# Slabs of four (entry, head) pairs interleaved by partition, with wq in the same ring of buffers

## The chip, the core and the metric

The kernel runs on one core of a Trainium2 chip. TensorE (PE) multiplies matrices, VectorE (DVE) and ScalarE (ACT) work element by element, GpSimd (POOL) only fills constants here, and SyncE (SP) issues the transfers from the chip's memory. A transfer is cut into packets, which 16 DMA engines carry. The core's SBUF has 128 partitions; matrix products land in PSUM. The metric is the device time of one execution in microseconds (us), lower is better.

## The reference

Two independent problems, A and B, have the same shapes, and their results stand side by side. Each is one decode step of attention over the last 4,096 positions of a cache, with 2 batch entries, 32 query heads and 16 key/value heads of 128 elements:

```python
W = min(4096, max(256, Sk // 4))                      # Sk = 16384
q = (x @ wq).reshape(B, Sq, Hq, Dh).transpose(0, 2, 1, 3)   # x: 2 x 1 x 576
k = jnp.repeat(k_cache[:, :, Sk - W:, :], rep, axis=1)      # rep = 2
v = jnp.repeat(v_cache[:, :, Sk - W:, :], rep, axis=1)
p = softmax(einsum("bhqd,bhkd->bhqk", q, k) * Dh ** -0.5)
o = einsum("bhqk,bhkd->bhqd", p, v)
return o.transpose(0, 2, 1, 3).reshape(B, Sq, Hq * Dh) @ wo   # wo: 4096 x 576
```

All arrays are bf16. K and V of the window are 134 MB of the 153.1 MB that the profile counts as read.

## The kernel before

Each (entry, head) pair needs 1 MB of K and 1 MB of V. A slab of 2 MB holds one key/value head for both entries: row `r` of 64 rows of 16 KB and entry `b` stand in partition `2r + b` (line 255). There are 32 slabs of K and 32 of V. They pass through a ring of 5 buffers (`NR`, line 77) in the order K0, K1, ..., K5, V0, K6, V1, ..., so that V runs `LS` = 5 slabs behind K (lines 227 to 231). Slab `s` takes buffer `s % 5` and waits for the last reader of slab `s - 5` (lines 258 to 260).

All loads but x stand in SP's queue in one fixed order, which `ensure_stream_until` (line 300) writes out. wq has buffers of its own, four loads of 1 MB in rows of 8 KB (line 282) and one of 0.5 MB (line 283). wo comes in 8 parts of 1,152 KB, one for each group of 8 pairs; a part fills `wob` with 128 rows of 9,216 bytes (lines 296 and 297), or for the last group with pieces of 1,152 bytes. The last V slab is cut into four pieces (`PIECES`, line 98).

For a K slab DVE transposes 32x32 blocks of 4-byte words, 512 words per partition at a time (line 844), and PE multiplies the result with `zq`, in which the queries stand so that each product adds into the right rows of a score bank (`fS`, line 867; its moving operand takes every fourth 2-byte element). After 8 units, that is 4 slabs, a group is complete: its maximum, exponent and sum pass through DVE, PE and ACT (`c_max` to `c_gather`, lines 373 to 493). V is multiplied four matmuls side by side, 16 columns of `pC` each (line 786); ACT or DVE copies the bank out (lines 802 and 804), PE adds its parts (line 758), DVE normalizes (line 561), and `redist`, `rev` and `gproj` (lines 630 to 665) apply wo. Every engine runs its instructions in the order in which the lists `S.add` were filled, and waits on semaphores for the others.

The new file is a rewrite of this plan with its own line numbers; these are given with the diff.

Of the kernel before, what the change touches and what calls it, by code (L numbers as in the profile page):

```python
# [59 lines left out]
def build_kernel(nc, probs, out, cfg=None):  # L60
    cfg = dict(cfg or {})
    NR = cfg.get("NR", 5)
    NKT = cfg.get("NKT", 3)
    NTB = cfg.get("NTB", 2)
    NZQ = 2
    ZW = 144
    LAG = cfg.get("LAG", 11)
    NPT = 3
    NS = cfg.get("NS", 56)
    LS = cfg.get("LS", 5)  # L70
    WQ_AT = cfg.get("WQ_AT", 7)
    QP_AT = cfg.get("QP_AT", 24)
    WO_LEAD = cfg.get("WO_LEAD", 5)
# [9 lines left out]
    NJ = W // 128  # L83
    assert NJ == 32
    NQ = 4
    NJ2 = 2 * NJ
    NRW = 64
    SLABW = NJ2 * 128
    UW = NJ * 128
    PP = Bb * Hkv  # L90
    NP = PP * NPROB
    ND = NP // 2
    NG = NP // 8
    GPP = PP // 8
    KP = PP // 2
    NK = NP // 2
    NFC = D // 128
    DREM = D - 128 * NFC
    assert DREM * 2 == 128
    HH = HD // 2  # L100
    NCH = NFC + 1
    NXC = NFC + 2
    NOUT = wo0.shape[1]
    NH = (NOUT + 1) // 2
    ACC0 = 128
    assert NOUT % 2 == 0 and ACC0 + NH <= 512 and NS <= 64 and NS % 2 == 0
    SCALE = float(Dh) ** -0.5
    PW = 512
    PIECES = [(0, 32), (32, 48), (48, 56), (56, 64)]

    def slab_info(D_):
        return D_ // Hkv, D_ % Hkv
# [5 lines left out]
    with es:  # L118
# [3 lines left out]
        xt = sb("xt", [128, NKT, UW], BF16)  # L122
        wqb = sb("wqb", [128, NFC, HD], BF16)
        wqr = sb("wqr", [128, HH], BF16)
        wob = sb("wob", [128, 2, 8, NOUT], BF16)
        xT = sb("xT", [128, NPROB, NXC, 64], BF16)
        x_dup = sb("x_dup", [Bb, NPROB, 2, DREM, 2], BF16)
        x_sb = sb("x_sb", [Bb, NPROB, D], BF16)
        ident_b = sb("ident_b", [128, 192], BF16)
        zq = sb("zq", [128, 4, NZQ, 8, ZW], BF16)  # L130
        pR = sb("pR", [128, 2, PW], BF16)
        pT = sb("pT", [128, 2, 2 * PW], BF16)
# [3 lines left out]
        sel = sb("sel", [128, 4, 128], BF16)  # L136
        qT_sb = sb("qT_sb", [128, NG, 64], BF16)
# [8 lines left out]
        oTn = sb("oTn", [128, 2, 2, Bb], BF16)  # L146
# [3 lines left out]
        maskS = sb("maskS", [128, 8], BF16)  # L150
        selL = sb("selL", [128, 240], BF16)
        acc_sb = sb("acc_sb", [128, 2, 512], BF16)
        ident_r = sb("ident_r", [128, 72], BF16)
        pC = sb("pC", [128, NPT, 4, 2, NJ, 4], BF16)
        mask_bh = sb("mask_bh", [128, Bb, 2], BF16)
        out_sb = sb("out_sb", [Bb, NPROB, NOUT], BF16)
        ps = lambda name, shape: es.enter_context(nc.psum_tensor(name, shape, FP32))
        TB = [ps("tb%d" % i, [128, 512]) for i in range(NTB)]
        assert NTB == 2
# [9 lines left out]
        x_sems = [sem("xload%d" % P) for P in range(NPROB)]  # L169
        out_sem = sem("outdone")  # L170
        lastq_sem = [sem("lastq%d" % q_) for q_ in range(4)]
# [10 lines left out]
        p_ones_b = S.add("pool", lambda e: e.memset(ones_b[:], 1.0), [], "ones_b")  # L182
        def f_identb(e):
            e.affine_select(ident_b[:, 0:128], ones_b[:], [[-1, 128]], ALU.is_equal, 0.0, base=0, channel_multiplier=1)
            return e.memset(ident_b[:, 128:192], 0.0)
        p_ident_b = S.add("pool", f_identb, [p_ones_b], "ident_b")
        p_zqT = S.add("pool", lambda e: e.memset(qT_sb[:].rearrange("d g w -> d (g w)"), 0.0), [], "zero_qT")
        p_zxT = S.add("pool", lambda e: e.memset(xT[:].rearrange("c p h w -> c (p h w)"), 0.0), [], "zero_xT")

        def zq_zero(eng, zr_, p4s, tag):  # L190
            ops_ = []
            for p4 in p4s:
                ops_.append(S.add(eng, lambda e, p4=p4: e.memset(zq[:, p4, zr_, :, :].rearrange("d l w -> d (l w)").bitcast(FP32), 0.0),
                                  [], "%s_%d" % (tag, p4)))
            return ops_
        p_zq = {0: zq_zero("pool", 0, (2, 3), "zero_zq0p")}

        def f_sel(e):
            last = None
            for p4 in range(4):  # L200
                b32, par = p4 // 2, p4 % 2
                last = e.affine_select(sel[:, p4, :].rearrange("d (a p) -> d a p", a=4), ones_b[:, :].rearrange("d (a p) -> d a p", a=4),
                                       [[0, 4], [-2, 32]], ALU.is_equal, 0.0, base=-(64 * b32 + par), channel_multiplier=1)
            return last
        p_sel = S.add("pool", f_sel, [p_ones_b], "sel")
        p_ones_f = S.add("pool", lambda e: e.memset(ones_f[:], 1.0), [], "ones_f")
        p_ident_f = S.add("pool", lambda e: e.affine_select(ident_f[:], ones_f[:], [[-1, 128]], ALU.is_equal, 0.0,
                                                           base=0, channel_multiplier=1), [p_ones_f], "ident_f")
        for zr_ in range(1, NZQ):
            p_zq[zr_] = zq_zero("pool", zr_, (0, 1, 2, 3), "zero_zq%d" % zr_)  # L210

        p_zq[0] = p_zq[0] + zq_zero("dve", 0, (0, 1), "zero_zq0d")
        init_zero = {}
        init_zero["ST0"] = S.add("dve", lambda e: e.memset(ST[0][:], 0.0), [], "zero_ST0")
        late_zero = [("ST1", ST[1]), ("OT0", OT[0]), ("OT1", OT[1]), ("ACC0", ACC[0]), ("ACC1", ACC[1])]

        x_sem = x_sems[0]

# [7 lines left out]
        stream = []  # L226
        for s_ in range(ND + LS):
            if s_ < ND:
                stream.append(("K", s_))
            if s_ >= LS:  # L230
                stream.append(("V", s_ - LS))
        slab_idx = {key: n for n, key in enumerate(stream)}
        w_at = {}
        for P in range(NPROB):
            t0 = 0 if P == 0 else WQ_AT + 4 * GPP * (P - 1)
            for ch in range(NCH):
                w_at.setdefault(t0 + (0 if P == 0 else ch), []).append(("wq", P, ch))
        for G in range(NG):
            w_at.setdefault(4 * G + LS + (2 if by_group(G) else -1), []).append(("wo", G, 0))

        slab_dma = {}
        slab_quarters = {}
        slab_last_reader = {}
        wq_dma = {}
        wo_dma = {}
        qproj = {}
        qproj_ev = {}
        proj = {}
        next_stream = [0]

        def issue_slab(s):
            kind, D_ = stream[s]
            P, g = slab_info(D_)
            src_t = probs[P][1] if kind == "K" else probs[P][2]
            src = src_t[:, g, Sk - W:Sk, :].rearrange("b (r j) d -> r b (j d)", r=NRW)
            r = s % NR
            deps = []
            if s >= NR:
                assert slab_last_reader.get(s - NR) is not None, ("ring too small / order", s)
                deps = [slab_last_reader[s - NR]]  # L260

            if s == len(stream) - 1:
                qops = []
                for n_, (ja, jb) in enumerate(PIECES):
                    def fq(e, r=r, src=src, n_=n_, ja=ja, jb=jb):
                        return e.dma_start(ring[:, r, ja * 128:jb * 128], src[:, :, ja * 128:jb * 128]).then_inc(lastq_sem[n_], 16)
                    qops.append(dma_op("sp", lastq_sem[n_], 1, fq, deps, "%s%d_q%d" % (kind, D_, n_)))
                slab_dma[s] = qops[-1]
                slab_quarters[s] = qops
                return  # L270

            def f(e, r=r, src=src):
                return e.dma_start(ring[:, r, :], src).then_inc(ring_sem[r], 16)
            slab_dma[s] = dma_op("sp", ring_sem[r], 1, f, deps, "%s%d" % (kind, D_))

        def issue_wq(P, ch):
            wqP = probs[P][3]
            deps = [qproj[P * GPP - 1]] if P >= 1 else []

            def f(e):  # L280
                if ch < NFC:
                    return e.dma_start(wqb[:, ch, :], wqP[ch * 128:(ch + 1) * 128, :]).then_inc(wq_sem[P], 16)
                return e.dma_start(wqr[:, :], wqP[NFC * 128:D, :].rearrange("r (h n) -> r h n", h=2)).then_inc(wq_sem[P], 16)
            wq_dma[(P, ch)] = dma_op("sp", wq_sem[P], 1, f, deps, "wq%d_%d" % (P, ch))

        def issue_wo(G):
            P = G // GPP
            Gl = G % GPP
            woP = probs[P][4]
            h0 = Gl * 8  # L290
            pc = G % 2
            deps = [proj[4 * (G - 2) + 3]] if G >= 2 else []

            def f(e):
                rows = woP[h0 * 128:(h0 + 8) * 128, :]
                src = rows.rearrange("(p s) n -> p s n", s=8) if by_group(G) else rows.rearrange("(h d) n -> d h n", d=128)
                return e.dma_start(wob[:, pc, :, :], src).then_inc(wo_sem[pc], 16)
# [42 lines left out]
        def group_of(i):  # L340
            return i // 8
# [652 lines left out]
```

## Time and profile before

| what | us |
|---|---|
| median of 3 runs | 372.18 (372.13 to 372.52) |
| the profiled execution, its own time | 373.62 |
| its span on the core | 371.8 |
| PE busy in the span | 313.2 |
| DVE busy in the span | 213.4 |
| ACT busy in the span | 30.4 |

The profile is of one execution. Its page cuts the span into 40 slices of 9.3 us and gives for each the share of time that engines were busy and the GB/s that the DMA engines moved. A group line gives the program line, the engine, the operation, the tiles and shapes, a count, the busy time, the mean of one in ns, and the idle time ahead with what ended it. "SPq" is SP's queue of transfers. The packet records of the trace hold start, duration and size of each packet; a semaphore's records hold when each part of a transfer reported that it had landed.

### The profile page before, as it was taken

The numbers are of one execution on the slowest core, as the hardware profiler recorded it, in microseconds if no ns is written. First come the engines' busy times: TensorE is split into PE (matmuls) and PEld (weight loads), VectorE is DVE, ScalarE is ACT, GpSimd is POOL, SyncE is SP. The second block draws the span as 40 slices with busy tenths as digits, with TensorE's granted clock in tenths as the row PEclk, the third lists the DMA queues.
The fourth block names the chain that finished last, engine by engine and source line by source line (L and its number), as shares of the span: only waits on it lengthen the run. The fifth ranks groups of instructions, "written<-read, shape, count | busy, mean of one in ns | idle before, by whom it ended". The sixth has DMA issues, their size and how long they took to land.

```text
span 371.8 us, 4249 instructions
## 1 busy us (share of the span) xinstructions
PE 313.2 (84%) x1764; PEld 97.3 (26%) x1764; DVE 213.4 (57%) x433; ACT 30.4 (8%) x99; POOL 6.5 (2%) x21
## 2 busy tenths in 40 slices
PE   0249997999899498999899878999699878998576
PEld 0214422222232134332223212322223222232132
DVE  3089638837853557545875557645775557726412
ACT  1100101010101001010101001010101001000111
POOL 7000000000000000000000000000000000000000
PEclk9998998999899699999989996999889996898769
DMA  7999999999999999999999999999999999999993
GB/s 310 435 430 428 427 420 361 391 386 434 420 435 428 427 425 427 420 429 428 430 429 421 428 434 425 422 432 427 425 427 430 425 427 427 425 429 413 434 414 120
DMA packets 13172, 153.39 MB, mean 413 GB/s; under 512 B 1368, under 2 KB 2400, under 8 KB 3040
## 3 DMA queue, kind: packets, MB, share of 16 engines
q1 hardware_dynamic: 13144, 153.10, 97.9%
q8 instruction: 14, 0.23, 0.3%
q14 instruction: 6, 0.05, 0.0%
q10 hardware_dynamic: 8, 0.00, 0.0%
HBM read 153.10 MB, written 0.00 MB: 412 GB/s over the span
## 4 chain that ended last, share of the span: by engine, by line
PE 46%; DMA 37%; DVE 13%; ACT 1%; issue 1%; SPq 1%
PE st L867 34%; DMA ring<-in_B_k_cache_dram 22%; DMA ring<-in_A_k_cache_dram 10%; DVE xt L844 8%; DMA ring<-in_B_v_cache_dram 5%; PE acc L786 4%; PE ot L658 3%; DVE pT L476 2%; PE tb L513 2%; DVE m L378 1%; DVE pC L491 1%; ACT pR L428 1%; PE tb L407 1%; PE tb L452 1%; PE tb L382 1%
## 5 line engine op out<-in xcount | busy, mean ns | idle before, releaser
L867 PE MATMUL st<-xt,zq 128*128 128x512 bf16 x512 | 236.0, 606 | 27.1 <-DVE xt L844 27.1
L844 DVE STREAM_TRANSPOSE xt<-ring 128x512 f32<-128x512 f32 x256 | 158.8, 675 | 53.5 <-DMA ring<-in_B_k_cache_dram 24.5
L867 PEld LDWEIGHTS st<-xt,zq 128*128 128x128 bf16 x512 | 48.9, 109 | 152.4 <-issue 108.2
L786 PE MATMUL acc<-ring,pC 128*16 128x512 bf16 x508 | 43.0, 412 | 3.5 <-DMA ring<-in_B_v_cache_dram 3.3
L561 DVE TENSOR_TENSOR oTg<-ot,rsb 128x4 bf16<-128x4 f32 x28 | 4.3, 152 | 38.0 <-PE ot L758 38.0
L802 ACT ACTIVATE acc_sb<-acc 128x512 bf16<-128x512 f32 x16 | 9.6, 597 | 143.0 <-PE acc L786 143.0
L804 DVE CAST acc_sb<-acc 128x512 bf16<-128x512 f32 x16 | 10.9, 678 | 15.1 <-PE acc L786 15.1
L476 DVE STREAM_TRANSPOSE pT<-pR 128x1024 bf16<-128x1024 bf16 x8 | 10.0, 1246 | 12.4 <-ACT pR L428 12.4
L513 PE MATMUL tb<-xT,wqb 128*128 128x56 bf16 x256 | 11.1, 198 | 6.5 <-DMA wqr<-in_A_wq_dram 6.5
L658 PE MATMUL ot<-wob,Rsb 128*2 128x288 bf16 x112 | 16.2, 302 | 0.3 <-ACT Rsb L646 0.3
L786 PEld LDWEIGHTS acc<-ring,pC 128*16 128x16 bf16 x508 | 7.9, 86 | 30.9 <-issue 23.8
L758 PEld LDWEIGHTS ot<-ident_r,acc_sb 128*128 128x128 bf16 x132 | 8.7, 106 | 20.8 <-issue 11.3
L513 PEld LDWEIGHTS tb<-xT,wqb 128*128 128x128 bf16 x256 | 10.8, 103 | 10.4 <-DMA wqr<-in_A_wq_dram 6.6
L658 PEld LDWEIGHTS ot<-wob,Rsb 128*2 128x2 bf16 x112 | 9.3, 88 | 10.1 <-issue 5.1
L378 DVE TENSOR_REDUCE m<-st 128x1 f32<-128x512 f32 x8 | 5.3, 667 | 9.7 <-PE st L867 9.7
L758 PE MATMUL ot<-ident_r,acc_sb 128*128 128x56 bf16 x132 | 9.7, 197 | 1.1 <-ACT out_sb L676 0.5
L513 PE MATMUL tb<-xT,wqr 128*128 128x56 bf16 x64 | 10.2, 197 | 0.0
L382 PE MATMUL tb<-ident_f,m 128*1 128x128 f32 x8 | 2.3, 283 | 8.6 <-DVE m L378 8.6
L545 ACT ACTIVATE zq<-tb 32x64 bf16<-32x64 f32 x32 | 7.1, 220 | 11.7 <-PE tb L527 11.5
L362 PE MATMUL tb<-ident_b,x_sb 2*128 2x2 bf16 x8 | 0.4, 161 | 7.5 <-DVE x_dup L348 7.5
L513 PEld LDWEIGHTS tb<-xT,wqr 128*128 128x128 bf16 x64 | 6.6, 103 | 0.0
L517 ACT ACTIVATE qT_sb<-tb 128x16 bf16<-128x16 f32 x8 | 1.5, 183 | 60.4 <-PE tb L513 60.4
(63 smaller groups left out, 84.6 us busy)
## 6 DMA issues: line engine op xcount, KB each, us to landing
ring<-in_A_k_cache_dram SPq DMA_DIRECT2D x16, 2048.0 KB, 18.0
ring<-in_A_v_cache_dram SPq DMA_DIRECT2D x16, 2048.0 KB, 16.7
ring<-in_B_k_cache_dram SPq DMA_DIRECT2D x16, 2048.0 KB, 17.6
ring<-in_B_v_cache_dram SPq DMA_DIRECT2D x15, 2048.0 KB, 19.0
wob<-in_A_wo_dram SPq DMA_DIRECT2D x4, 1152.0 KB, 17.1
wob<-in_B_wo_dram SPq DMA_DIRECT2D x4, 1152.0 KB, 16.9
wqb<-in_A_wq_dram SPq DMA_DIRECT2D x4, 1024.0 KB, 7.9
wqb<-in_B_wq_dram SPq DMA_DIRECT2D x4, 1024.0 KB, 15.7
```

The lines of the kernel that those rows point to most:

```text
L378: chain[(G, "max")] = S.add("dve", lambda e: e.tensor_reduce(m1[:], ST[x][:, :], AX.X, ALU.max), deps, "cmax_%d" % G)
L382: n, bank, op = tb_job(lambda e, bank: e.transpose(bank[0:1, 0:128], m1[:, 0:1], ident_f[:]), "cTm_%d" % G, [chain[(G, "max")], p_ident_f])
L476: return e.transpose(pT[:, G % 2, :], src)
L513: last = e.matmul(bank[:, hl * 64:hl * 64 + NS], w_, x_, start=(ch == 0), stop=(ch == NCH - 1))
L545: last = e.activation(dst, src, ACTF.Copy)
L658: last = e.matmul(OT[half][0:Bb, ACC0:ACC0 + NH], Rsb[:, G % 2, s_, :], wob[:, G % 2, s_, half * NH:(half + 1) * NH], start=False, stop=Tr ...
L758: last = e.matmul(OT[x][:, 0:NS], acc_sb[:, x, 128 * jl4:128 * jl4 + 128], ident_r[:, 4 * jl4:4 * jl4 + NS], start=False, stop=True, skip_ ...
L786: last = e.matmul(ACC[x][32 * cb:32 * cb + 16, 0:512], pC[:, pr, gl, jh, jl:jl + 4, :].rearrange("k j c -> k (j c)"), ring[:, r, j0_ * 128 ...
L802: acc_ev[D_] = S.add("act", lambda e: e.activation(acc_sb[:, x, :], ACC[x][:, :], ACTF.Copy), d, "accev_%d" % D_)
L804: acc_ev[D_] = S.add("dve", lambda e: e.tensor_copy(acc_sb[:, x, :], ACC[x][:, :]), d, "accev_%d" % D_)
L844: xop = S.add("dve", lambda e, r=r, c=c, q=q, o=o: e.transpose(xt[:, c, q * 1024:(q + 1) * 1024].bitcast(FP32), ring[:, r, o:o + 1024].bit ...
L867: last = e.matmul(ST[x][:, 0:512], zq[:, p4, zr, 2 * gl + b, 16 - 16 * jh:144 - 16 * jh], mv, start=False, stop=True, skip_group_check=True)
```

## The change

Slabs are now 4 MB and hold four pairs: heads `g` and `g + 8` of both entries. Row `r` of 32 rows of 32 KB and pair `c` stand in partition `4r + c`. There are 16 slabs of K and 16 of V, V two slabs behind K, in a ring of 3 buffers. The first 512 rows of wq also come through this ring, as one load of 4 MB, ahead of K0 for A and ahead of K3 for B; the buffers `wqb` are gone.

The transposition takes 1,024 words per instruction and writes each pair to a place of its own, so consecutive words that it writes lie 2,048 bytes apart (`[128, 2, 2, 4, 64, 8]`, the fourth index is the pair). The matmul for the scores then reads every second 2-byte element of one pair. q is projected with x as the stationary operand and 512 columns of wq moving, and is brought into place by a DVE transposition and copies. A group is two slabs; because the groups now hold heads from the two halves of the 32 query heads, a part of wo is two runs of 512 rows, half of wo apart. As built, the source of this load is 2 by 64 rows of 4,608 elements, its destination 128 partitions; before, both sides were 128 by 4,608. The last part of wo is two loads. PV uses 32 columns of `pC`; only ACT copies its bank out. The last V slab is cut into five pieces. The output leaves in four transfers.

```diff
-    NR = cfg.get("NR", 5)
-    LS = cfg.get("LS", 5)
+    NR = cfg.get("NR", 3)
+    LS = 2
+    WQ_AT = cfg.get("WQ_AT", 3)
...
-    PIECES = [(0, 32), (32, 48), (48, 56), (56, 64)]
+    PIECES = [(0, 64), (64, 96), (96, 112), (112, 120), (120, 128)]
...
-        xt = sb("xt", [128, NKT, UW], BF16)
-        wqb = sb("wqb", [128, NFC, HD], BF16)
+        xt = sb("xt", [128, 2, 2, 4, 64, 8], FP32)
...
+        for s_ in range(ND + LS):
+            if s_ == 0 or s_ == WQ_AT:
+                stream.append(("Q", 0 if s_ == 0 else 1))
+            if s_ < ND:
+                stream.append(("K", s_))
+            if s_ >= LS:
+                stream.append(("V", s_ - LS))
+        for G in range(NG):
+            s_ = 2 * G + LS if by_group(G) else 2 * G + 1
+            w_at.setdefault(("K", s_) if s_ < ND else ("V", s_ - LS), []).append(G)
...
-            src = src_t[:, g, Sk - W:Sk, :].rearrange("b (r j) d -> r b (j d)", r=NRW)
-            r = s % NR
+            src = src_t.rearrange("b h s d -> (b h) s d")[g::SPP, Sk - W:Sk, :].rearrange("c (r j) d -> r c (j d)", r=32)
+            r = n % NR
+            deps = [reader[n - NR]] if n >= NR else []
...
+        def issue_wq(n, P):
+            deps = [reader[n - NR]] if n >= NR else []
+            slab_dma[n] = dma_op("sp", ring_sem[r], 1, lambda e: e.dma_start(
+                ring[:, r, :], wqP[0:NFC * 128, :].rearrange("(p s) n -> p (s n)", s=NFC)).then_inc(ring_sem[r], 16), deps, "wq%d" % P)
...
         def issue_wo(G):
-            deps = [proj[4 * (G - 2) + 3]] if G >= 2 else []
-                rows = woP[h0 * 128:(h0 + 8) * 128, :]
-                src = rows.rearrange("(p s) n -> p s n", s=8) if by_group(G) else rows.rearrange("(h d) n -> d h n", d=128)
-                return e.dma_start(wob[:, pc, :, :], src).then_inc(wo_sem[pc], 16)
+            deps = [proj[2 * (G - 2) + 1]] if G >= 2 else []
+                if by_group(G):
+                    src = woP.rearrange("(t r) n -> t r n", t=2)[:, r0:r0 + 512, :].rearrange("t (p s) n -> t p (s n)", s=8)
+                    return e.dma_start(wob[:, pc, :, :].rearrange("p s n -> p (s n)"), src).then_inc(wo_sem[pc], 16)
+                for t in range(2):
+                    src = woP[t * HH + r0:t * HH + r0 + 512, :].rearrange("(h d) n -> d h n", d=128)
+                    last = e.dma_start(wob[:, pc, 4 * t:4 * t + 4, :], src).then_inc(wo_sem[pc], 16)
...
+        def do_X(s, u):
+                    src = ring[:, n % NR, o:o + 4096].bitcast(FP32).rearrange("k (j f w) -> k f j w", f=2, w=32)[:, hf]
+                    dst = xt[:, bf, hf, :, 32 * q:32 * q + 32, :].rearrange("k c j r -> k j r c")
+                    return e.transpose(dst, src)
+        def do_S(s, u):
+                        mv = xt[:, bf, hf, c, :, :].rearrange("k j r -> k (j r)").bitcast(BF16).rearrange(
+                            "k (n t) -> k n t", t=2)[:, :, par]
...
+        for s in range(ND + 1):
+            D2 = s - 3
...
+                for c in range(NU):
+                    do_X(s, c)
+                    if c >= 1:
+                        do_S(s, c - 1)
...
+                    if D2 >= 0:
+                        if c == 0:
+                            do_comb(D2)
+                        elif c == 1:
+                            do_norm(D2)
+                        elif c == 2 and D2 % 2 == 1:
+                            do_redist(D2 // 2)
+                        elif c == 3 and D2 % 2 == 1:
+                            do_proj(D2)
...
+                    if s == WQ_AT:
+                        do_qproj(GPP + c)
+                do_S(s, NU - 1)
+                if s % 2 == 1:
+                    do_max(s // 2)
+                    do_exp(s // 2)
+                if s >= LS:
+                    do_PV(s - LS, range(NRD), None)
+                if s % 2 == 1:
+                    do_sum(s // 2)
```

In the new file the slab load is line 231, that of wq line 238, the parts of wo lines 253 and 257, the pieces line 228, the transposition line 410 and the score matmul line 433.

## The prediction

> **What bounds the kernel now.** I read the slices first, then the transfer queues, the transfers one kind at a time, the waits of SP's queue, and the groups of instructions.
>
> ```profile
> DMA  7999999999999999999999999999999999999993
> DMA packets 13172, 153.39 MB, mean 413 GB/s; under 512 B 1368, under 2 KB 2400, under 8 KB 3040
> q1 hardware_dynamic: 13144, 153.10, 97.9%
> ...
> L867 PE MATMUL st<-xt,zq 128*128 128x512 bf16 x512 | 236.0, 606 | 27.1 <-DVE xt L844 27.1
> L844 DVE STREAM_TRANSPOSE xt<-ring 128x512 f32<-128x512 f32 x256 | 158.8, 675 | 53.5 <-DMA ring<-in_B_k_cache_dram 24.5
> ...
> L658 PE MATMUL ot<-wob,Rsb 128*2 128x288 bf16 x112 | 16.2, 302 | 0.3 <-ACT Rsb L646 0.3
> ```
>
> The 16 DMA engines are full in every slice but the first and the last: packets take 97.9% of 371.8 us, 364.0 us on each engine, and 7.8 us are left for the head and the tail. The chain of waits gives PE 46%, but PE and DVE wait for slabs (24.5 us of DVE's idle time ahead of L844 is K of B), not the slabs for them. So what counts is the work of the fullest DMA engine, plus the time in which it has nothing issued.
>
> ```profile
> wob<-in_A_wo_dram SPq DMA_DIRECT2D x4, 1152.0 KB, 17.1
> wob<-in_B_wo_dram SPq DMA_DIRECT2D x4, 1152.0 KB, 16.9
> ...
> out_dram<-out_sb SPq DMA_DIRECT2D x2, 2.2 KB
> x_sb<-in_A_x_dram ACTq DMA_DIRECT2D x1, 2.2 KB
> ```
>
> The second line of the first fence counts 1,368 packets under 512 B. They are the reports of landing. There are 85 transfers with 128 rows (63 slabs, 4 pieces, 10 parts of wq, 8 of wo) and 4 with two rows (x and the output): 85 x 16 + 4 x 2 = 1,368. So a transfer does not always use 16 engines: these four used two each, and the landing records of their semaphores say the same. The packet records give the prices: 620 ns on average for 16,384 B (median 613), 319 for 8,192, 351 for 9,216, 161 for 4,096, 85 for 2,048, 51 for 1,152.
>
> **The change, on the transfers.** Slabs: 31 whole ones, each 8 packets of 32 KB per engine. No row has such a packet. As two of 16 KB it costs 1,240 ns; growing as the medians do from 309 to 613 it costs 613 + 2 x 304 = 1,221. I take 1,240, since hardware may cut it in two: 31 x 8 x 1.240 = 307.5 us (302.8 by the other). The five pieces: 8 x (0.620 + 0.319 + 0.161 + 2 x 0.085) = 10.2. wq: 2 x 8 x 1.240 = 19.8, its rest 2 x 8 x 0.161 = 2.6. The last part of wo: 64 x 0.051 = 3.3. Reports: about 0.5. That is 343.9 us per engine, without the seven other parts of wo.
>
> Those seven are what I expect to decide. Before, a part was 128 rows on 16 engines: 8 x 0.351 = 2.8 us each. Now its source is 2 by 64 rows, while the destination still counts 128 partitions. Every other large load keeps 32 or 128 in front, and 64 in front (the old slabs) used 16 engines. The lower bound is that 128 partitions decide, 2.8 us; the upper one is that the 2 in front decides, as in x and the output, the only rows with a 2 in front: 64 rows on each of two engines, 64 x 0.351 = 22.5 us. I take the upper one, the row it is nearest to in what differs. Then two engines carry 7 x 22.5 = 157.2 us of wo instead of 19.7, and in all 343.9 + 157.2 = 501.1 us. Every slab needs all 16 engines, so these two set the pace.
>
> [...]
>
> Two engines now write into all 128 partitions, where the other 14 land their slabs. In the trace each engine always delivers about 26 GB/s (16,384 B in 620 ns) to its own 8 of the 128 rows, so it does not say whether the engine or the partitions limit this. Bounds for a wo packet beside moving slabs: 351 ns, or 702 if two writers share one writer's rate. The slots say how long the others move during a part: after it starts on the slow engines they get V (K's slot free after X) and then K (V's slot free after PV), 2 x 9.9 = 19.8 us. Shared fully a part takes about 9 us more, not shared 0. I take 550 ns in those stretches, nearer to 702 because no row shows more than that rate into a partition group: in 19.8 us then go packets worth 19.8 x 351 / 550 = 12.6 us, so a part takes 7.2 us more, 50 us in all.
>
> [...]
>
> **Waits on the transfer queue.** Nothing waits while the two slow engines have work queued. Between two parts they carry four slabs, 4 x 9.9 = 39.7 us, and a part: a period of 62 us or more, eight periods. K's next slot needs 8 transpositions of 1,024 words. Four of 512 take 2.49 us in the timeline, so 1.24 each, 9.9 us; writing words 2,048 bytes apart is in no row, and the nearest with a step is L867, 0.432 us apart against 0.227 for 512 contiguous columns (L658: 16 x 288 in 2.05 us), a factor of 1.9: at most 2.4 each, 19 us. I take 1.24. Either fits into the two slabs queued behind it. V's slot needs the scores (32 matmuls x 0.432 = 13.8 us, half of that if a step of two runs full speed) and PV (32 x 0.085 = 2.7), which is in time too.
>
> One wait is not covered. The last part of wo (before K15) waits for `proj(11)`, which PE reaches only after the third quarter of S(14), and K15 stands behind it in SP's queue. From the end of K14 on the engines: 1.5 us landing, 9 to 15 us of transposition and scores, 2 of projection, 1.5 to start, against 9.9 us of V12 queued: 4.6 to 12, I take 6. The wait of K4 for the last q projection of B (its slot holds wq) is hidden by the 22.5 us of the part of wo ahead of it; without that cover it costs 5 to 10 us.
>
> **The change, on the engines.** DVE per period: 16 x 1.24 = 19.8, transposing P doubles to 2 x 1.246, masks 4 x 0.40, the rest some 2: 26 us. PE: 64 x 0.432 = 27.6, PV 5.4, others about 5: 38. The q projection replaces 320 matmuls by 80 with 512 columns, some 0.23 each: 18 us for 21. All of it stays under 62 us. Without that cover (a period of 42.5) PE still fits, and DVE at its upper bound, 38 + 6, would not. The memsets of banks that go, and the second queue for the output (up to 0.5 us), I cost at nothing: the tail of 7.8 us with the head is kept.
>
> **Sum:** 501.1 + 7.8 + 6 + 50 = 565 us of span against 371.8. The profiled execution took 373.62, the median 372.18; the span is within 0.4 of the median, so I say 565.
>
> **Rivals.**
> *Two engines, no sharing:* 501.1 + 7.8 + 6 = 515. For it: every 9,216 B packet took about 351 ns. Against: none was in a shared place.
> *Sixteen engines carry wo:* 343.9 + 19.7 + 7.8 + 6 + 8 for K4's wait = 385, from 372 with the waits covered to 400 (DVE at 2.4 us a piece needs 44 us per period instead of 42.5, 8 x 1.5 us more). For it: the destination has 128 partitions. Against: the count of reports.
> *Not slower:* sixteen engines, packets of 32 KB at 1,221 ns and the waits for K4 and the last wo covered, because the score matmul at a step of two runs at 0.227 us. Mechanism: large packets save 4.7 us of slab time; it decides if the two waits together stay under some 5 us. 302.8 + 36.4 + 19.7 + 7.8 = 366.7, with 4 us of waits 371. Against: SP's order, which puts K15 behind `proj(11)`.
>
> **How the numbers follow.** Two engines with sharing 0.55, without 0.28; sixteen with waits 0.12, sixteen with waits covered 0.05. The predicted time is the first, 565. The range, 505 to 600, holds both cases of two engines and their bounds (501.1 falls to 496 with 1,221 ns; 63 + 12 on top give 584, with DVE late some more); the sixteen-engine cases stay outside. Within 0.2% a measurement of this kernel cannot be told from no change. Faster 0.03, same 0.02 (both out of the last case), slower 0.95.
>
> **What would show it.** The parts of wo: time to landing far above 17 us, two landings instead of 16 per part, so 7 x 14 = 98 fewer small packets. The mean DMA share falls to about 65%, with transfers at full rate only part of each period; DVE's wait for K slabs grows by some 150 us. Packets of 9,216 B above 351 ns mean sharing. If wo lands with 16 reports, or its packets end within 3 us, the forecast is wrong; if L410 takes over 4 us, DVE bounds the kernel instead and the time exceeds the range.

## The result, and the profile after

The changed kernel took 642.2 us (median of 4 runs, 641.2 to 644.1) beside 372.35 us for the kernel before on the same chip: a ratio of 1.7235, 95% interval 1.7168 to 1.7303. Its profiled execution took 644.1 us, of which 642.4 are the span. The forecast was 565 with a range of 505 to 600: the side and the place were right, the size fell 77 us short.

First the slices and the queues of the changed kernel's page:

```profile
DMA  9999817559859991399922999319994199613993
GB/s 370 443 266 261 291 54 310 248 157 316 345 220 289 253 273 78 149 348 259 267 89 110 360 258 254 132 77 387 256 235 158 50 389 250 160 57 129 439 418 141
DMA packets 7764, 153.31 MB, mean 239 GB/s; under 512 B 698, under 2 KB 1734, under 8 KB 2374
q1 hardware_dynamic: 7738, 153.10, 71.8%
```

A row of full slices is now broken seven times by slices in which few engines move anything. The GB/s of the kernel before, in slices of 9.3 us, have no such breaks:

```profile
GB/s 310 435 430 428 427 420 361 391 386 434 420 435 428 427 425 427 420 429 428 430 429 421 428 434 425 422 432 427 425 427 430 425 427 427 425 429 413 434 414 120
```

The same 153.10 MB are moved. But 71.8% of 642.4 us is 461 us of packet time per engine, against 364 us before: the engines are not only idle more, their packets also take longer. Small packets number 698; the same kernel with 16 engines for each part of wo (the first experiment) has 796. The difference is 98 = 7 x 14, so seven transfers report from two engines instead of 16. The semaphore records agree: per part, one update comes at once and two at the landing (for the first part at 4.0 us, then at 71.6 and 76.1 us).

Next the transfers of the changed kernel, one kind a line: count, KB each, median us from issue to landing.

```profile
ring<-in_A_k_cache_dram SPq DMA_DIRECT2D x8, 4096.0 KB, 40.8
...
ring<-in_B_k_cache_dram SPq DMA_DIRECT2D x8, 4096.0 KB, 61.5
...
wob<-in_A_wo_dram SPq DMA_DIRECT2D x4, 1152.0 KB
...
wob<-in_B_wo_dram SPq DMA_DIRECT2D x3, 1152.0 KB
```

A slab of 4 MB takes 9.7 us at the full rate (8 packets of 1,213 ns per engine), but K of B lands 61.5 us after its issue, as it is queued behind a part of wo on two engines. For the parts themselves the page gives no landing time.

The waits say who is late (engine, tile and line waiting, what it waited for: us in total, times, longest):

```profile
PE st L433 <- DVE xt L410: 349.1, 50, 43.0
...
DVE xt L410 <- DMA ring<-in_B_k_cache_dram: 176.0, 8, 39.0
...
DVE xt L410 <- DMA ring<-in_A_k_cache_dram: 106.7, 6, 39.7
```

The same waits in the kernel before:

```profile
DVE xt L844 <- DMA ring<-in_B_k_cache_dram: 24.5, 12, 3.5
DVE xt L844 <- DMA ring<-in_A_k_cache_dram: 23.7, 4, 11.9
```

PE waits for DVE, and DVE for K: 176.0 + 106.7 = 282.7 us instead of 24.5 + 23.7 = 48.2, in stretches of up to 39.7 us, one or two for each part of wo. It is the transfers, not the engines, that set the time. The window of one part, 267 to 312 us, shows the worst of it (busy us of each engine, then the granted clock, the DMA share and GB/s):

```profile
core 0: us, PE busy (x) PEld busy (x) DVE busy (x) ACT busy (x) POOL busy (x), PEclk, DMA share, GB/s
...
267.00:312.00 45.00, 16.87 (x116) 6.46 (x118) 19.94 (x19) 3.24 (x10) 0.00 (x0) 0.76 0.99 296
```

All DMA engines are busy 99% of the time and yet move 296 GB/s, not the 425 or so of most slices of the kernel before. A busy share says that packets are under way, not how fast. The packet records, in steps of 3 us, show which are slow (`...` stands for steps left out):

```
start us   wo packets   mean ns    32 KB packets   mean us
276.8           3         347           35           1.23
279.8          10         538           35           1.36
282.8           8         678           21           2.31
...
291.8          10         681           21           2.24
...
312.8           9         663           20           2.20
...
318.8           4         661           33           1.36
321.8           3         670           14           1.35
324.8           0          -             7           1.22
```

While two engines carry wo, their 9,216 B packets take about 680 ns instead of 351, and the 32 KB packets of the other 14 engines take about 2.2 us instead of 1.2.

### The profile page after: what moved, and what is told of

Its sections match the earlier page's. It is cut to its first block, busy times and chain, and to the rows that moved or that the text cites. A ratio compares the mean times of both kernels' runs of the same rounds, so it can differ in the third digit from the quotient of the medians.

```text
span 642.4 us, 3369 instructions
## 1 busy us (share of the span) xinstructions
PE 224.4 (35%) x1401; PEld 88.9 (14%) x1424; DVE 289.0 (45%) x284; ACT 39.2 (6%) x107; POOL 5.7 (1%) x10
## 3 DMA queue, kind: packets, MB, share of 16 engines
q1 hardware_dynamic: 7738, 153.10, 71.8%
HBM read 153.10 MB, written 0.00 MB: 238 GB/s over the span
## 4 chain that ended last, share of the span: by engine, by line
DVE 36%; another core or an unknown queue 35%; DMA 14%; PE 8%; issue 5%; ACT 2%; SPq 0%
DVE xt L410 29%; DMA ring<-in_A_k_cache_dram 10%; PE st L433 3%; DVE pT L479 3%; DMA ring<-in_B_k_cache_dram 2%; DMA wqr<-in_A_wq_dram 2%; PE tb L354 2%; DVE pC L489 1%; PE acc L534 1%; DVE m L442 1%; ACT pR L474 1%; PE ot L637 1%; PE tb L461 0%; DVE qtr L368 0%
## 5 line engine op out<-in xcount | busy, mean ns | idle before, releaser
L410 DVE STREAM_TRANSPOSE xt<-ring 128x1024 f32<-128x1024 f32 x128 | 232.3, 1931 | 283.0 <-DMA ring<-in_B_k_cache_dram 176.0
L433 PE MATMUL st<-xt,zq 128*128 128x512 bf16 x492 | 147.1, 446 | 352.7 <-DVE xt L410 349.1
L534 PE MATMUL acc<-ring,pC 128*32 128x512 bf16 x508 | 33.1, 396 | 0.0
L479 DVE STREAM_TRANSPOSE pT<-pR 128x2048 bf16<-128x2048 bf16 x8 | 18.5, 2312 | 11.9 <-ACT pR L474 11.9
L354 PE MATMUL tb<-ring,xT 128*128 128x512 bf16 x62 | 18.6, 425 | 8.6 <-DMA wqr<-in_A_wq_dram 5.4
L534 PEld LDWEIGHTS acc<-ring,pC 128*32 128x32 bf16 x508 | 13.9, 99 | 13.9 <-issue 4.2
L362 ACT ACTIVATE qrow<-tb 128x512 bf16<-128x512 f32 x16 | 9.4, 597 | 36.0 <-PE tb L354 34.1
L489 DVE TENSOR_TENSOR pC<-pT,maskC 128x1024 bf16<-128x1024 bf16 x16 | 10.4, 688 | 0.3
L637 PE MATMUL ot<-wob,Rsb 128*2 128x288 bf16 x112 | 8.9, 307 | 0.3 <-ACT Rsb L615 0.3
L392 ACT ACTIVATE zq<-qk 32x64 bf16<-32x64 bf16 x32 | 8.2, 255 | 1.6 <-DVE qk L376 1.2
## 6 DMA issues: line engine op xcount, KB each, us to landing
ring<-in_B_k_cache_dram SPq DMA_DIRECT2D x8, 4096.0 KB, 61.5
```

Source lines behind the costliest of these rows:

```text
L354: last = e.matmul(bank[:, 0:512], x_, w_, start=(ch == 0), stop=(ch == NFC))
L362: evs.append(S.add("act", lambda e, bank=bank, nb=nb: e.activation(qrow[:, 512 * nb:512 * nb + 512], bank[:, 0:512], ACTF.Copy), d, "qrow% ...
L392: last = e.activation(dst, qk[pr_, G, :, :, :], ACTF.Copy)
L410: return e.transpose(dst, src)
L433: last = e.matmul(ST[G % 2][:, 0:512], zq[:, 2 * hf + par, zr, 4 * sl + c, w0:w0 + 128], mv, start=first and c == 0 and par == 0, stop=fin ...
L479: chain[(G, "pT")] = S.add("dve", lambda e: e.transpose(pT[:].rearrange("k j w -> k (j w)"), pR[:, G % 2, :].rearrange("m (j r) -> m j r", ...
```

## The experiments

**1. Rows in front.** The source of the part is turned round, so that 64 rows stand ahead of the two halves; the bytes are the same, and the lookup of the rows in `selL` follows.

```diff
-  src = woP.rearrange("(t r) n -> t r n", t=2)[:, r0:r0 + 512, :].rearrange("t (p s) n -> t p (s n)", s=8)
+  src = woP.rearrange("(t r) n -> t r n", t=2)[:, r0:r0 + 512, :].rearrange("t (p s) n -> p t (s n)", s=8)
```

> The seven parts of wo are loaded with the 64 rows in front of the 2 halves (64 by 2 by 4,608 elements instead of 2 by 64 by 4,608), and the constant that spreads the rows is moved to match; nothing else is changed. Theory (two engines carry wo and slow the other fourteen): 16 landings per part, packets of 9,216 B back at about 351 ns, packets of 32 KB at 1,213 ns throughout, and a span of 336.8 (slabs and wq at 1,213 ns) + 19.7 + 7.8 + 6 for the last part of wo + some 12 for K4 behind the q projection = 382 us, 372 to 400. Rival (the ring of three 4 MB slabs with the transposition at 1.81 us a piece starves the engines): the time stays above 500 us. Rival (packets of 32 KB are slow beside any other transfer): 32 KB packets of 2.2 us remain.

It took 413.6 us, ratio 1.1075 (1.1035 to 1.1114). One turned index gives back 229 of the 270 us. Wo packets take 349 ns on average, 32 KB packets 1,241 (median 1,213). But it is some 31 us above the 382 expected, and above the expected range too. Its slices of 10.3 us show where:

```profile
DMA  8999869089389999999999999999999998199990
```

The windows of the same kernel give the stretches (columns as above):

```profile
40.00:120.00 80.00, 46.28 (x219) 17.48 (x224) 59.33 (x61) 8.29 (x20) 0.00 (x0) 0.87 0.67 277
120.00:340.00 220.00, 129.13 (x811) 49.88 (x818) 173.15 (x148) 16.83 (x56) 0.00 (x0) 0.84 0.99 420
340.00:360.00 20.00, 11.10 (x88) 4.83 (x80) 18.65 (x16) 1.72 (x5) 0.00 (x0) 0.83 0.51 219
```

From 120 to 340 us the transfers are nearly as full as in the kernel before, 99% and 420 GB/s. What is lost lies in the start (a share of 0.67 of the 80 us from 40 to 120, so some 26 us) and around 355 us (7 us without any transfer, the last part of wo).

**2. The part of wo alone.** The changed kernel with its two engines, but the slab behind each of the seven parts is issued only once the part has landed. It adds a wait and takes nothing away.

```diff
-            deps = [reader[n - NR]] if n >= NR else []
+            deps = ([reader[n - NR]] if n >= NR else []) + behind
...
                     issue_wo(G)
+                    behind[:] = [wo_dma[G]] if by_group(G) else []
```

> The parts of wo stay on two engines, but the slab behind each of them in SP's queue waits until the part has landed, so that a part moves nearly alone. Theory (the loss is that wo and slabs slow each other where they move together): packets of 9,216 B at about 350 ns, packets of 32 KB at about 1,213 ns, each part 22.5 us instead of the 37 to 45 of the changed kernel, and although a wait is added the span falls to 336.8 + 7 x (22.5 + 3) + 7.8 + 6 = 529 us, 515 to 560. Rival (a part on two engines takes 45 us by itself): 336.8 + 7 x (45 + 3) + 14 = 687 us, slower than the changed kernel.

It took 531.2 us (531.1 to 531.4), ratio 1.4234 (1.4176 to 1.4292), 111 us less than the changed kernel. The slices and the queue on its page:

```profile
DMA  8951799922999139971499616994179921959993
...
q1 hardware_dynamic: 7738, 153.10, 68.1%
```

The waits of SP's queue in it (us in total, times, longest; line 759 is the wait itself):

```profile
SPq L759 <- DMA wob<-in_A_wo_dram: 164.8, 4, 52.0
...
SPq L759 <- DMA wob<-in_B_wo_dram: 105.8, 3, 35.3
```

SP now waits 270.6 us for wo in all, and the kernel is faster: 68.1% of 529.6 us is 361 us of packet time per engine, so the 100 us of longer packets (461 - 361) are gone. Wo packets take 347.5 ns here. Nothing else was changed, so moving slabs beside wo costs at least these 111 us (the new waits cost something too), where the forecast had 50.

**3. Two loads of 64 rows.** Each part is two loads, each into 64 partitions, with 64 rows in front.

```diff
+  for t in range(2):
+      src = woP[t * HH + r0:t * HH + r0 + 512, :].rearrange("(p s) n -> p (s n)", s=8)
+      last = e.dma_start(wob[64 * t:64 * t + 64, pc, :, :].rearrange("p s n -> p (s n)"), src).then_inc(wo_sem[pc], 16)
...
```

> Each of the seven parts of wo becomes two loads of 64 rows into 64 partitions each; the rest is as in the changed kernel. Theory (the number in front of the source decides): 16 landings per load, and about the time of the kernel with the rows in front, 382 us. Where two writers into the same group of partitions share one writer's rate, the 16 engines that write 64 partitions take about 700 ns for a packet of 9,216 B instead of 351, which is 7 x 2.8 = 20 us more, 402 us. Rival (ring and transposition starve the engines): above 500 us.

It took 430.9 us, ratio 1.1553 (1.1504 to 1.1602), 17 us above the first experiment, where about 20 were expected. With 64 rows in front, as in the first experiment, 16 engines are taken to carry wo here too, but into 64 partitions at a time, and a 9,216 B packet takes 670 ns instead of 349. So the number of rows in front is not all: between these two runs it is where the packets land that differs, and the time is near the 700 ns expected if two writers share one writer's rate. The 32 KB packets that ran beside these loads took some 1.9 us.

**4. Sharing by itself.** Transfers only, no attention: slabs go through the ring, and beside them small loads of wo by two engines at a time, first into partitions taken to be those that the two engines' own slab rows fill (the packet records do not name partitions), then 8 and 64 partitions away (`p0` below is 0, 8 and 64), then over all 128. It was run once.

```diff
+  p = p0 + 32 * (j // 4) + j % 4
...
+  e.dma_start(scr[p:p + 5:4, :, :], wo[:, 8 * i:8 * i + 8:2, :]).then_inc(pair_sem[j], 16)
```

> A kernel of transfers alone, which leaves out all of the computation: 42 slabs of 4 MB run three deep on SP's queue, and beside slabs 7, 14, 21, 28 and 35 ACT issues 64 rows of 9,216 B on each of two engines: into partitions 0 to 3 and 32 to 35 with their neighbours four further on; the same 8 further; the same 64 further; into all 128 partitions as in the changed kernel; and at last the same 128 rows with 64 in front, on 16 engines. Theory (an engine's slab packets slow only while the second writer is at the same partitions): the first three sets slow the slab packets of two engines each to some 2.2 us and leave the others at 1.21, and the fourth slows each engine for a part of the time, some 1.35 us on average over all. Rival (a transfer on two engines of itself halves the rate of all): about all slab packets at 2.2 us in all four sets. Rival (only the spread over the partitions does it): the first three sets slow few, the fourth slows all.

The GB/s of its page, 40 slices of 13.6 us:

```profile
GB/s 352 430 454 425 425 430 431 448 425 426 425 431 433 345 357 299 304 314 318 318 318 318 318 321 314 318 318 318 318 315 316 314 308 333 317 286 311 94 51 111
```

| loads beside the slabs | window, us | 32 KB packet, mean ns | GB/s |
|---|---|---|---|
| none | 10 to 80 | 1,215 | 433 |
| into the engines' own partitions | 85 to 177 | 1,218 | 433 |
| 8 partitions away | 199 to 320 | 1,443 | 311 |
| 64 partitions away | 325 to 448 | 1,442 | 313 |
| over all 128, two engines | 454 to 510 | 1,393 | 294 |

Loads into the own partitions leave the slabs' packets as they were. (The set ends at 193 us; from 177 us on the rate falls to 343 GB/s while the median packet stays at 1,213 ns, which the author reads as pauses of the others for the two engines that are behind.) Loads elsewhere slow the packets of far more than two engines: the medians of the sets 8 and 64 partitions away are 1,468 and 1,480 ns, so more than half of all slab packets are slow. The GB/s of these sets hold such pauses too. None of the stated theories says that. The last set, 16 engines, began when the slabs had ended and tells nothing. The loads here moved only some 5.5 GB/s per engine, so the size is not that of the kernel; the kind of it is. Why so many engines become slow was not settled.

**5. Contiguous transposition.** The first experiment's kernel, but the transposition writes its words in order, and the score matmul takes one pair out of the four with a step of 16 bytes.

```diff
-  xt = sb("xt", [128, 2, 2, 4, 64, 8], FP32)
+  xt = sb("xt", [128, 2, 2, 64, 8, 4], FP32)
...
-  dst = xt[:, bf, hf, :, 32 * q:32 * q + 32, :].rearrange("k c j r -> k j r c")
+  dst = xt[:, bf, hf, 32 * q:32 * q + 32, :, :]
```

> On top of the kernel with the rows in front, the transposition writes its words side by side, the four pairs interleaved, and the score matmul reads one 2-byte element in eight instead of one in two. Theory (the transposition takes 1.81 us instead of 1.24 because its words go 2,048 bytes apart, and this starves the ring in the first 120 us): 1.24 us a piece, score matmuls 0.43 us apart instead of 0.23, and the 30 us that the engines idle between 40 and 120 us shrink to about 15: 413 - 15 = 398 us, 385 to 410. Rival (the price is that of the four-dimensional pattern, not of the place written): 1.81 us stays, and the slower matmuls add to 413.

It took 651.3 us, ratio 1.744 (1.7392 to 1.7488). Its groups:

```profile
L433 PE MATMUL st<-xt,zq 128*128 128x512 bf16 x512 | 465.5, 1077 | 23.6 <-DVE xt L410 23.6
L410 DVE STREAM_TRANSPOSE xt<-ring 128x1024 f32<-128x1024 f32 x128 | 147.8, 1206 | 83.1 <-DMA ring<-in_B_k_cache_dram 36.1
```

The transposition falls to 147.8 / 128 = 1.15 us, but a matmul rises to 465.5 / 512 = 0.91 us and PE bounds the kernel. The low granted clock of this run (0.576) does not explain it: the few of these matmuls that ran while the clock was granted in full (37 of them) also started 0.90 us apart. The expectation failed: with a step of 16 bytes PE, where 512 matmuls pay it, loses far more than DVE gains.

**6. The last part of wo later.** The first experiment's kernel with the last part of wo behind K15 in SP's queue instead of ahead of it.

```diff
-  w_at.setdefault(("K", s_) if s_ < ND else ("V", s_ - LS), []).append(G)
+  w_at.setdefault(("K", s_) if by_group(G) else ("V", s_ - LS), []).append(G)
```

> On top of the kernel with the rows in front, the last part of wo is issued behind K15 instead of ahead of it. Theory (K15 stands behind the wait of that part for the projection of slab 11, and the engines idle for 7.1 us at 353 us): 413.6 - 7 = 406.5 us, 404 to 409. Rival (the wait only moves to V13): 413.

It took 402.4 us, ratio 1.0754 (1.0708 to 1.08): 11 us less than the first experiment, and a little below the 404 to 409 expected. The hole is gone from its slices of 10 us:

```profile
DMA  8999779159629999999999999999999999989993
```

The wait of the last part was real. The 4 us beyond the hole of 7 were not looked into.

**7. Two words side by side.** The sixth kernel with an `xt` in which two pairs stand side by side, so that DVE writes two words in order and PE reads with a step of 8 bytes.

```diff
-  xt = sb("xt", [128, 2, 2, 4, 64, 8], FP32)
+  xt = sb("xt", [128, 2, 2, 2, 64, 8, 2], FP32)
```

> On top of the kernel with the rows in front and the last part of wo later: the transposition writes two words side by side and the other two pairs 4,096 bytes further, and the score matmul reads every fourth 2-byte element, as before the change. Theory (DVE pays for each place that does not follow the last one, PE for each step over 4 bytes): 1.4 to 1.6 us a transposition instead of 1.81, 0.43 us a score matmul instead of 0.25; PE has room for it, so the first 120 us lose some 8 us less: 402 - 8 = 394 us. Rival (PE becomes the bound as with 16 bytes): above 402.

It took 398.4 us, ratio 1.0676 (1.0641 to 1.0711), only 4 us less than the sixth, where 8 were expected. Its groups:

```profile
L433 PE MATMUL st<-xt,zq 128*128 128x512 bf16 x512 | 236.1, 630 | 23.2 <-DVE xt L410 23.2
L410 DVE STREAM_TRANSPOSE xt<-ring 128x1024 f32<-128x1024 f32 x128 | 147.2, 1207 | 51.0 <-DMA ring<-in_A_k_cache_dram 33.2
```

Two words in order already give DVE the time of the fifth experiment, where all are in order: 147.2 / 128 = 1.15 us (1.4 to 1.6 had been expected). PE pays 236.1 / 512 = 0.46 us.

**8. The projections of q early.** The sixth kernel, but the q projections of A stand between the transpositions of K0, the constants come first, and B's q projections go ahead of the transpositions of K3, so that the buffer with wq comes free sooner.

```diff
+                if s == WQ_AT:
+                    for c in range(NU):
+                        do_qproj(GPP + c)
                 for c in range(NU):
                     do_X(s, c)
                     if c >= 1:
                         do_S(s, c - 1)
+                    if s == 0 and c + 1 < GPP:
+                        do_qproj(c + 1)
```

> On top of the kernel with the rows in front and the last part of wo later: three of the first q projections stand behind pieces of the first transposition instead of ahead of all, the small constants ahead of them, and the four q projections of B stand ahead of the transposition of K3. Theory (the ring of three, in which wq holds a slot, idles the engines for 30 us between 40 and 120 us, because its slots wait for DVE and for the last q projection): the first slot comes free some 5 us earlier and K4's wait goes, 402 - 10 = 392 us, 386 to 398. Rival (DVE alone sets the first 85 us, so order does not matter): 399 or more.

It took 392.3 us, ratio 1.0518 (1.0492 to 1.0544), 10 us less than the sixth and as expected. Three of its windows:

```profile
60.00:80.00 20.00, 9.54 (x30) 3.44 (x30) 18.05 (x16) 1.13 (x4) 0.00 (x0) 0.74 0.50 213
...
100.00:340.00 240.00, 145.39 (x919) 55.61 (x918) 197.09 (x172) 19.28 (x61) 0.00 (x0) 0.87 0.99 423
340.00:360.00 20.00, 12.87 (x92) 4.85 (x90) 15.48 (x12) 0.78 (x2) 0.00 (x0) 0.87 1.01 410
```

The one large hole left is at 60 to 80 us: DVE is busy 18 of the 20 us, 13 of them with transpositions of K, and the next slab waits for a buffer that it has yet to read.

**9. Seventh and eighth together.** The order of the eighth kernel with the `xt` of the seventh.

```diff
-  xt = sb("xt", [128, 2, 2, 4, 64, 8], FP32)
+  xt = sb("xt", [128, 2, 2, 2, 64, 8, 2], FP32)
```

> Both of these edits together. Theory: the gains add while the start is bound by DVE: 402 - 18 = 384 us, 376 to 392; still above 372, since the engines' work of 356.5 us, 8 us of head and tail and what is left of the start stand against 364 + 8 before. Rival (a gain of one is hidden by the other): 390 or more.

It took 395.2 us, ratio 1.0588 (1.0567 to 1.061), 3 us more than the eighth. The expected gain did not come. Its windows beside those of the eighth:

```profile
60.00:80.00 20.00, 12.04 (x30) 3.60 (x29) 14.20 (x16) 1.13 (x4) 0.00 (x0) 0.74 0.63 256
...
100.00:340.00 240.00, 208.57 (x908) 61.23 (x907) 136.68 (x168) 19.27 (x61) 0.00 (x0) 0.86 0.99 417
340.00:360.00 20.00, 19.29 (x96) 5.52 (x95) 12.82 (x17) 0.78 (x2) 0.00 (x0) 0.97 0.80 324
```

The hole at 60 to 80 us shrinks only from 10 to 7.4 us (a share of 0.63 instead of 0.50). In the middle 417 GB/s are moved instead of 423, and from 340 to 360 us 4 us of transfers are lost that the eighth did not lose. PE is busy 208.6 of the 240 us in the middle and 19.3 of the 20 after it, beside 145.4 and 12.9; that it sets the time there is likely, but was not tested. No version that was run is faster than the kernel before.

## Why the prediction was right in kind and wrong in size

**Two engines: right.** The reports (two per part, 98 fewer small packets) and the first experiment, which undoes just this and takes 229 us off, show it. With 2 in front of the source the changed kernel has two landings for each part and 698 small packets in all; with 64 in front the first experiment has 796, which is 16 for each part.

**Sharing: this step failed.** The forecast had a wo packet at 550 ns during 19.8 us of each part, and so 50 us in all. It let only the wo packets grow, and took the slabs beside them as moving on at their old rate. (Its price for full sharing, about 9 us per part, is 9.9 by its own terms, 19.8 x (1 - 351 / 702); that is not what was missing.) The trace shows 680 ns for the one and 2.2 us for the other: a neighbour that is itself slowed stays beside the part twice as long, and the two terms multiply. With 16 packets of 2.2 us on each of the 14 engines the stretch is 35 us, not 19.8, and 35 x (1 - 351 / 680) = 17 us are lost per part, 119 in all. The second experiment, which takes the sharing away and adds waits, gains 111 us and ends at a span of 529.6, as was worked out for it.

Counted on the packets themselves, the mean of wo over seven parts is 604 ns, 64 x 0.604 = 38.7 us per engine and part, 270.5 in all, where the forecast had 207.2: 63 of the 77 us. From the first to the last packet the parts took 37 to 45.5 us, 298 us together: the two engines do not run side by side, and their landings of a part are 3.7 to 7.4 us apart. The remaining 14 us are not itemised. After six of the parts a single engine has the last 3.3 to 3.9 us to itself, 21.6 us in all, which the forecast did not have; how much of that is loss is not shown.

The upper bound of the forecast was 702 ns, two writers at one writer's rate; the third experiment's 670 ns for loads into 64 partitions, about twice 349, comes near it. But read that way, only the engines whose partitions are being written would be slow (which engine fills which was taken, in the forecast too, and is in no packet record). In the kernel all are, at one time: from 282.8 to 285.8 us the fastest of the 21 32 KB packets took 2.19 us. In the fourth experiment more than half of the packets are. So why the slabs of the other engines slow down stays open; that they do, and what it costs, is shown.

**Packets of 32 KB: nearly right.** 1,213 ns alone, where 1,240 was taken and 1,221 was the other bound: 264 x 27 ns = 7 us too much. That such a packet is cut in two, the reason given for 1,240, is not shown: the packet records hold 4,224 of 32,768 B.

**The last part of wo: right in the changed kernel.** The engines have nothing to move from 583.0 to 589.2 us, 6.2 us where 6 was taken. The 1.5 us for landing and the 1.5 to start that went into it were the author's estimates: the trace has 0.44 us from the last report's packet to its landing, at 583.0 us, and 1.06 from SP's issue of the part at 588.14 us to the first packet. The sixth experiment shows that moving it gains 11 us where the engines are otherwise full.

**The transposition: inside its bounds, above the value taken.** 232.3 / 128 = 1.81 us instead of 1.24 (bound 2.4):

```profile
L410 DVE STREAM_TRANSPOSE xt<-ring 128x1024 f32<-128x1024 f32 x128 | 232.3, 1931 | 283.0 <-DMA ring<-in_B_k_cache_dram 176.0
```

Its 283 us of idle time say that it did not decide the changed kernel. Once wo has 16 engines it has a part: in the first experiment DVE is busy 59 of the 80 us in which transfers are lost, but making it cheaper gained only 4 us (the seventh).

**The score matmul.** The timeline of the changed kernel (start, us, engine, operation, count, idle time before) has eight in a row:

```profile
263.67 1.98 PE L433 MATMUL st<-xt,zq 128*128 128x512 bf16 x8 [1.83 <-DVE xt L410]
```

That is 0.247 us each, the end of the last one included. Over the whole trace the starts of such matmuls lie 0.226 us apart (median) where the clock is granted in full, and 0.427 where half of it is. So a step of two (4 bytes) costs nothing against the 0.227 of the forecast at the full clock, and the lower of the two values holds there. The step of four (8 bytes) is another matter: its 0.431 us in the kernel before and 0.451 in the seventh are the same at either clock.

**The rivals.** "Two engines, no sharing", 515, has its counterpart in the second experiment, 531, with the added waits. "Sixteen engines carry wo" was put at 385, 372 to 400; the first experiment says 413.6. What it lacked is the start: with three buffers, one of them held by wq, the next slab waits for transpositions of 1.81 us and for the q projections. It had 8 us for this; some 26 are seen between 40 and 120 us, and the eighth experiment gets 10 of them back by order alone. "Not slower" asked for full speed at a step of two, which holds, and for covered waits, which do not.

**The signs given.** The DMA share was to fall to about 65%, and is 71.8% because longer packets count as busy; DVE's wait for K was to grow by 150 us and grew by 234.5.

## What to carry to other kernels

When a load is rewritten, read how many engines its reports come from; two engines out of 16 on loads of 1,152 KB held up what was queued behind them here, 642.2 us against 413.6 with 16. Where a transfer on few engines runs beside others, as wo did here, price both sides at the slower rate that was measured (680 ns instead of 351 and 2.2 us instead of 1.2), and lengthen the time that they share accordingly; if the small one must be narrow, letting it go alone can be the cheaper order (531.2 us here). A high DMA share beside a low rate in GB/s is the sign to look for: 99% and 296 GB/s from 267 to 312 us, where most slices of the kernel before have some 425.

## What the runs showed of the hardware

Loads on two engines beside the slabs slowed the slabs' packets: in the changed kernel, where 14 engines move slabs, from 1,213 to some 2,200 ns, and in the fourth experiment, transfers alone, from 1,215 to 1,443 and 1,442 ns on average when the loads went 8 and 64 partitions away from those taken to be the two engines' own. Into those taken to be their own they left the packets at 1,218.

The 128x512 bf16 score matmuls whose moving operand has a step of 4 bytes start 0.226 us apart at the full granted clock and 0.427 at half of it (the changed kernel). With 8 bytes it is 0.431 us in the kernel before and 0.451 in the seventh experiment, and with 16 bytes 0.90 in the fifth, at either clock.

A DVE transposition of 1,024 words takes 1.15 us when it writes in order (the fifth experiment) or in runs of two words (the seventh), and 1.81 us when consecutive words lie 2,048 bytes apart (the changed kernel).
